# Where the first expert's weights are loaded among attention's loads

## The chip, the cores and the metric

The kernel runs on one core of a Trainium2 chip. The metric is device time in microseconds (us) of one execution, given as the median over the runs.

## What is computed

An mLSTM cell over 4 batches, 8 heads, 768 positions and head size 40, and behind it a layer of 8 experts to which each position is sent by a hash of its token. All is float32. The reference, cut:

```python
for t in range(S):                       # per batch and head
    m_new  = maximum(f_gate[t] + m, i_gate[t])
    f_stab = exp(f_gate[t] + m - m_new); i_stab = exp(i_gate[t] - m_new)
    C = f_stab * C + i_stab * outer(v[t], k[t])
    n = f_stab * n + i_stab * k[t]
    y[t] = sigmoid(o_gate[t]) * (C @ q[t]) / maximum(abs(n @ q[t]), 1.0)
x = y.transpose(0, 2, 1, 3).reshape(3072, 320)
expert = token_ids * 2654435761 % 8
for e in range(8):
    out[expert == e] = maximum(x[expert == e] @ w1[e], 0) @ w2[e]   # w1[e] 320x1024, w2[e] 1024x320
```

## The kernel before, in words

The 3072 positions are 24 tiles of 128; tile s belongs to batch s % 4 and chunk s // 4. Attention is one loop over 24 steps (L810). It is written under a manual schedule: each engine carries out its instructions in the order in which the program names them, and so does SyncE with the loads that it issues.

The recurrence is done by chunks. For a tile, PE turns k and q (`turn`, L390), multiplies them to scores (`scores`, L447), and makes the decays from the gate rows R and the row ends L (`decays`, L405, and xb, L418). ACT takes their exponential (L414), DVE multiplies scores and decays (`weigh`, L453). `state` (L478) makes the chunk's part of the state C, `attend` (L499 and L505) the output, which DVE divides (`divided`) and POOL multiplies with the output gate (`gated`, L522). ACT works out the output gate (`gate`, L438 and L439).

The work is staggered: step s turns tile s + 2, makes the scores and decays of tile s + 1 and attends tile s. The gate of tile i is worked out in step i + 1 for i of 8 and more.

SyncE's queue holds nearly all loads. In step s, in this order: the gate rows R of tile s + 3 (`load_a`, L248; 24 KB, three buffers), k and q of tile s + 5 and v of tile s + 4 (L237; 160 KB each, in pieces of 160 bytes, six buffers each), in each fourth step the ends L, the output gate og of tile s + 1 (L233; 160 KB, pieces of 160 bytes; early in the loop sometimes two of them), and the stores of finished rows x (L525; 160 KB). Then come the "pieces" of the step (L846): small parts of the routing, and the loads of the first expert's weights. From tile 17 on, the x rows are stored from POOL's queue.

`slices_of(0)` (L120) makes seven pieces for the first expert's weights: two halves of w1t (512 KB each, 128 rows of 4 KB; L131), w1c (two loads of 128 KB; L134), and four slices of w2t (320 KB each; L137). Their tiles belong to expert 0 alone at this time, so nothing has to be free before they are loaded. Behind the loop, L901 uses w1t and w1c (`layer1` of the rows of two gathered tiles, L157 and L150), and the second block uses w2t (`layer2`, L1030).

After attention, POOL gathers the rows of each expert from the stored x, the rows go through `x_slots` to the turned blocks, and the experts 1 to 7 follow, each with its own loads of weights (L97 to L101).

Of the kernel before, what the change touches and what calls it, by code (L numbers as in the profile page):

```python
# [22 lines left out]
def kernel(  # L23
# [96 lines left out]
    def slices_of(e):  # L120

        w1t = wpools[0].tile([P, 2, F], F32, name="w1t")
        w1c = wpools[0].tile([P, FB // 2, P], F32, name="w1c")
        w2t = w2pools[0].tile([P, FB, Dm], F32, name="w2t")
        W[e] = w1t, w1c, w2t
        last = moe_w1[e][2 * P :, :].rearrange("d (a two f) -> two d a f", two=2, f=P)
        rows = moe_w2[e].rearrange("(a p) d -> p a d", p=P)

        def part(i):
            if i < 2:  # L130
                nc.sync.dma_start(w1t[:, i], moe_w1[e][i * P : (i + 1) * P, :])  # L131
            elif i == 2:
                for j in range(2):
                    nc.sync.dma_start(w1c[j * P // 2 : (j + 1) * P // 2], last[j])  # L134
            else:
                r = slice(2 * (i - 3), 2 * (i - 2))
                nc.sync.dma_start(w2t[:, r], rows[:, r])  # L137

        return [lambda i=i: part(i) for i in range(7)]
# [50 lines left out]
    with tc.tile_pool(name="gates", bufs=1) as gp, \  # L190
# [363 lines left out]
        def route_iotas(i):  # L554
            for ti, tf, pattern, base, mult in list(iotas.values())[i::2]:
                nc.gpsimd.iota(ti[:], pattern=pattern, base=base, channel_multiplier=mult)
                nc.gpsimd.tensor_copy(tf[:], ti[:])
# [140 lines left out]
        def route_table(i):  # L698
            tk = ps.tile([P, 2, NC], F32, name="tk", tag="sp0")
            for t in range(TH):  # L700
                nc.tensor.matmul(tk[:], lhsT=oh_r[:, t, :], rhs=oh_c[:, t], start=(t == 0), stop=(t == TH - 1))
            for part in range(2):
                if i == 0 and part == 0:
                    nc.vector.tensor_copy(tv[:], tk[:, 0])
                else:
                    nc.vector.tensor_tensor(tv[:], tv[:], tk[:, part], op=ALU.add)

        def route_index():
# [17 lines left out]
        pieces = {  # L726
            2: [lambda: route_iotas(0)], 3: [lambda: route_iotas(1), route_consts, route_parts], 4: [route_experts],
            5: [route_chosen], 7: [route_extra, route_masked], 8: [route_rank], 9: [route_high], 10: [route_slots, g2.ends, lambda: g2.split("e")], 11: [route_places],
            20: [route_index], 21: [route_tiles],
        }  # L730
        products = {4: [route_turned], 5: [route_counts]}
        for i in range(8):
            pieces.setdefault(12 + i, []).append(lambda i=i: route_hot(i))
            if i % 2:
                products[12 + i] = [lambda i=i // 2: route_table(i)]
        for i, part in enumerate(slices_of(0)):
            pieces.setdefault(17 + i, []).append(part)
        gates_of = {}
        for i, j in enumerate((4, 5, 6, 6, 7, 8, 8, 9)):
            gates_of.setdefault(j, []).append(i)  # L740
# [356 lines left out]
    with tc.manual_schedule():  # L1097
# [56 lines left out]
        for e in range(E):  # L1154
            g, i = e // EG, e % EG
# [84 lines left out]
```

## Time and profile before

| | us |
|---|---|
| median of 6 runs | 357.03 (354.9 to 361.04) |
| profiled execution, its own time | 359.1 |
| its span, first to last instruction | 357.1 |
| PE busy | 338.6 (95%) |
| DVE, ACT, POOL busy | 226.8, 138.4, 213.7 |
| attention's loop, about | 10 to 130 |
| first layer of expert 0 | 130 to 140 |
| experts 1 to 7 | 162 to 337 |

Time is counted from the start of the span. In a timeline or chain, a line holds the start, the duration, the engine and line number; "SPq" is an issue in SyncE's queue, "DMA" a transfer's flight, "issue" time in which the profile shows no wait. In square brackets stands the idle time before an instruction and what ended it. A table by stretches of time gives the busy time of PE, PE's weight loads, DVE, ACT and POOL, then the granted PE clock (1.00 is full), the DMA share of the 16 engines and the GB/s. The DMA share sums the time of packets, which can overlap, so it can pass 1.

The trace also keeps each transfer's semaphore events: each DMA engine that takes part counts one up when its part has landed.

### The profile page before, as it was taken

To read this page: it belongs to the slowest core of one execution; us is meant where nothing else is said; L and a number is where in the kernel's file an instruction comes from. 1 tells how busy PE (TensorE), PEld (TensorE's weight loads), DVE (VectorE), ACT (ScalarE), POOL (GpSimd) and SP (SyncE) were. 2 spreads that over 40 slices of the span, in tenths; PEclk is the share of its full clock that TensorE was granted. 3 is DMA by queue.
4 is the path that set the end of the run, shared out by engine and by line. 5 is a ranking of instruction groups with operands and counts; after the bars stand their busy time and mean duration, and the time that the engine had idled before them with its cause. 6 is when DMAs were issued, how large, how long until landed. Compare 5 with 4: busy or idle time off the path is not lost.

```text
span 357.1 us, 9206 instructions
## 1 busy us (share of the span) xinstructions
PE 338.6 (95%) x3573; PEld 291.8 (82%) x3573; DVE 226.8 (64%) x512; ACT 138.4 (39%) x325; POOL 213.7 (60%) x301
## 2 busy tenths in 40 slices
PE   6889999999999799999999999999999999999990
PEld 5677898888888677788899899689899899898870
DVE  8867897998888551056765786826666757645310
ACT  6676688776675351113213212212313212213200
POOL 8832778899885546407717938816917829329221
PEclk9999999999999899999999999999999999999997
DMA  6699999999999963689878869495585592010010
GB/s 128 116 174 172 174 187 176 194 190 184 172 181 245 228 203 110 174 230 288 239 208 238 272 104 366 107 247 177 118 239 194 115 265 99 0 37 19 17 39 3
DMA packets 162358, 59.18 MB, mean 166 GB/s; under 512 B 140171, under 2 KB 158119, under 8 KB 162313
## 3 DMA queue, kind: packets, MB, share of 16 engines
q1 hardware_dynamic: 158377, 49.05, 59.0%
q0 software_dynamic: 2832, 9.34, 8.0%
q8 instruction: 29, 0.48, 0.6%
q10 hardware_dynamic: 1104, 0.18, 0.3%
q14 instruction: 16, 0.13, 0.1%
HBM read 46.48 MB, written 12.38 MB: 165 GB/s over the span
## 4 chain that ended last, share of the span: by engine, by line
PE 77%; DMA 6%; issue 5%; DVE 4%; SPq 3%; POOL 2%; ACT 1%; ACTq 0%; POOLq 0%; DVEq 0%
PE mh L988 20%; PE mh L1063 13%; PE zp L1030 8%; PE mh L996 6%; PE sp L447 6%; PE tr L390 5%; PE xh L505 5%; PE xh L499 3%; PE ab L405 3%; PE xh L478 2%; SPq L1125 2%; DMA R<-gate_rows 2%; DMA w1t<-in_moe_w_dram 2%; PE zp L1143 1%; DMA xg<-x_rows,g_idx 1%
## 5 line engine op out<-in xcount | busy, mean ns | idle before, releaser
L914 POOL DMA_INDIRECT out_dram<-zo,s_idx x26 | 27.3, 1051 | 76.7 <-issue 47.1
L1030 PE MATMUL zp<-w2t,h 128*128 128x320 f32 x160 | 45.0, 433 | 0.5 <-ACT h L166 0.5
L974 DVE TENSOR_TENSOR h<-u,mh 128x416 f32<-128x416 f32 (+1 forms) x56 | 25.5, 475 | 25.0 <-PE mh L988 12.7
L1030 PEld LDWEIGHTS zp<-w2t,h 128*128 128x128 f32 x160 | 30.0, 190 | 11.8 <-ACT h L166 0.9
L505 PE MATMUL xh<-v,w 128*64 128x41 f32 x768 | 35.7, 226 | 0.0
L414 ACT ACTIVATE w<-ab 128x512 f32<-128x512 f32 x48 | 26.2, 596 | 19.6 <-PE ab L405 18.7
L453 DVE TENSOR_TENSOR w<-sp,w 128x512 f32<-128x512 f32 x48 | 30.8, 682 | 3.8 <-ACT w L414 3.8
L988 PE MATMUL mh<-tx,sw 128*128 128x208 f32 x168 | 31.9, 340 | 0.5 <-DVE sw L944 0.5
L505 PEld LDWEIGHTS xh<-v,w 128*64 128x64 f32 x768 | 31.8, 141 | 0.0
L988 PEld LDWEIGHTS mh<-tx,sw 128*128 128x128 f32 x168 | 29.7, 190 | 0.9 <-DVE sw L944 0.9
L447 PE MATMUL sp<-qT,kT 64*128 64x128 f32 x384 | 28.3, 286 | 1.1 <-ACT qT L395 1.1
L110 POOL DMA_INDIRECT xg<-x_rows,g_idx x24 | 23.3, 972 | 9.0 <-issue 6.7
L499 PE MATMUL xh<-C,qs 128*64 128x82 f32 x320 | 28.2, 254 | 0.0
L447 PEld LDWEIGHTS sp<-qT,kT 64*128 64x128 f32 x384 | 23.7, 189 | 5.0 <-issue 2.5
L1063 PE MATMUL mh<-tw,sh 128*128 128x160 f32 x168 | 27.4, 299 | 0.0
L522 POOL TENSOR_TENSOR x<-x,og 128x320 f32<-128x320 f32 x24 | 20.6, 864 | 10.4 <-ACT og L439 8.3
L974 DVE TENSOR_TENSOR u<-m,mh 128x416 f32<-128x416 f32 x28 | 16.5, 588 | 13.3 <-ACT m L1002 6.8
L1012 ACT ACTIVATE h<-mh 128x416 f32<-128x416 f32 x14 | 7.2, 518 | 44.3 <-PE mh L996 44.3
L1063 PEld LDWEIGHTS mh<-tw,sh 128*128 128x128 f32 x168 | 24.3, 190 | 0.0
L988 PE MATMUL mh<-xT,w1t 128*128 128x208 f32 x112 | 24.3, 339 | 0.0
L996 PE MATMUL mh<-xT,w1c 64*128 64x208 f32 x224 | 23.5, 349 | 0.0
L488 POOL TENSOR_TENSOR C<-C,add 64x164 f32<-64x164 f32 x32 | 16.3, 508 | 9.9 <-ACT add L482 8.7
(241 smaller groups left out, 758.1 us busy)
## 6 DMA issues: line engine op xcount, KB each, us to landing
w2t<-in_moe_w_dram SPq DMA_DIRECT2D x7, 1280.0 KB
w1t<-in_moe_w_dram SPq DMA_DIRECT2D x7, 1024.0 KB
xb<-x_slots SPq DMA_DIRECT2D x84, 52.0 KB
k<-in_k_dram SPq DMA_DIRECT2D x24, 160.0 KB
v<-in_v_dram SPq DMA_DIRECT2D x24, 160.0 KB
og<-in_o_gate_dram SPq DMA_DIRECT2D x24, 160.0 KB
q<-in_q_dram SPq DMA_DIRECT2D x23, 160.0 KB
x_slots<-xg SPq DMA_DIRECT2D x7, 480.0 KB
```

The costliest lines, as they stand in the source:

```text
L110: nc.gpsimd.indirect_dma_start(out=xg, out_offset=None, in_=x_d[:rows, :], in_offset=bass.IndirectOffsetOnAxis(ap=idx, axis=0),)
L414: nc.scalar.activation(w[:, hf], ab[:], AF.Exp)
L447: nc.tensor.matmul(sp[hf][:, j, :], lhsT=d["kT"][r, j, :], rhs=d["qT"][r, j, :], start=True, stop=True)
L453: nc.vector.tensor_tensor(d["w"][:, hf], d["sp"][hf][:], d["w"][:, hf], op=ALU.mult)
L499: nc.tensor.matmul(xh[t, 2 * j : 2 * j + 2, :], lhsT=d["qs"][:, j, t], rhs=Cs[b][c % 2][:, j].rearrange("p h d -> p (h d)"), start=True, s ...
L505: nc.tensor.matmul(hs[t, 2 * j + hf, :], lhsT=d["w"][:, hf, j, t], rhs=d["v"][:, 2 * j + hf, :], start=(c == 0), stop=True, skip_group_che ...
L914: ins = nc.gpsimd.indirect_dma_start(out=out[:, :], out_offset=bass.IndirectOffsetOnAxis(ap=idx, axis=0), in_=zo[:], in_offset=None, bound ...
L974: nc.vector.tensor_tensor(o, a, b, op=ALU.add)
L988: nc.tensor.matmul(pair(bank[n])[:, a], lhsT=lhsT(g + a), rhs=rhs, start=first and a == 0, stop=True, skip_group_check=True,)
L996: nc.tensor.matmul(pair(bank[n])[:, a], lhsT=w1c[k, g + a, :], rhs=xT[k, 2, r], start=False, stop=True, skip_group_check=True,)
L1030: nc.tensor.matmul(zp[:], lhsT=h[:, fb, j * P : (j + 1) * P], rhs=w[2][:, fb, :], start=(fb == 0), stop=(fb == FB - 1),)
L1063: nc.tensor.matmul(bank[n], lhsT=lhsT(f), rhs=rhs(f), start=first and f == 0, stop=f == FB // 2 - 1, skip_group_check=True,)
```

## The change

The seven pieces go to other steps: the two w1t halves from steps 17 and 18 to 2 and 9, w1c from 19 to 15, and the four w2t slices from 20, 21, 22 and 23 to 21, 21, 22 and 22. In SyncE's queue this puts the first w1t half ahead of tile 6's R, the second ahead of tile 13's, w1c ahead of tile 19's, and all w2t slices behind the last og load. The order of the instructions on ACT and POOL stays the same.

```diff
-        for i, part in enumerate(slices_of(0)):
-            pieces.setdefault(17 + i, []).append(part)
+        for s, part in zip((2, 9, 15, 21, 21, 22, 22), slices_of(0)):
+            pieces.setdefault(s, []).append(part)
```

## The prediction

> **What bounds it now.** I read the page first (PE is busy 95% of the span and holds 77% of the chain), then the chain of waits, because the edit touches only SyncE's queue and matters only where a transfer ends a PE wait. In all of attention the waits of PE name one such place; the chain, around it:
>
> ```profile
> 110.78 0.47 PE tr L390 x4
> ...
> 112.35 0.51 SPq L233
> ...
> 112.96 0.59 SPq L525
> ...
> 113.61 0.47 SPq L131
> ...
> 114.17 5.42 DMA R<-gate_rows
> 119.59 0.04 issue
> 119.64 0.62 PE ab L405 x4
> ```
>
> Here PE, in step 21, waits for the gate rows R of tile 22. They were issued at 114.17, straight behind the second w1t slice (L131), and took 5.42 us to land. PE's timeline puts the price on it, and the table by stretches shows what comes after:
>
> ```profile
> 115.96 1.27 PE L447 MATMUL sp<-qT,kT 64*128 64x128 f32 x16
> 119.64 0.62 PE L405 MATMUL ab<-R,L 128*64 128x512 bf16 x4 [2.40 <-DMA R<-gate_rows]
> ...
> 124.53 0.62 PE L405 MATMUL ab<-R,L 128*64 128x512 bf16 x4
> ```
>
> ```profile
> 118.00:119.60 1.60, 0.00 (x0) 0.00 (x0) 0.43 (x3) 0.00 (x0) 1.10 (x2) 1.00 0.85 194
> ...
> 121.60:122.60 1.00, 1.00 (x22) 1.00 (x21) 0.88 (x2) 0.71 (x2) 0.17 (x1) 0.50 0.87 157
> ```
>
> After 2.40 us of idle the granted clock (the third column from the right) is 0.50. From decays to the end of attend, step 20 took 2.25 us (112.69 to 114.94) and step 21, at half clock, 3.60 (119.64 to 123.24): 1.35 more; the following scores take 1.29 in the chain where others take 1.09: 0.20 more. So the stall costs 2.40 + 1.35 + 0.20 = **3.95 us**, all on the chain. No other wait of PE stands between 35 and 126 us.
>
> The second thing to know is how full the transfers are before that:
>
> ```profile
> 30.00:55.00 25.00, 24.82 (x481) 21.22 (x479) 22.32 (x58) 18.13 (x45) 16.51 (x25) 1.00 0.98 178
> 55.00:80.00 25.00, 25.00 (x500) 21.93 (x498) 22.42 (x49) 19.47 (x50) 22.20 (x41) 1.00 0.93 189
> 80.00:105.00 25.00, 25.00 (x500) 21.94 (x496) 20.80 (x53) 16.94 (x41) 21.95 (x37) 1.00 0.93 182
> 105.00:130.00 25.00, 22.14 (x400) 19.28 (x396) 17.94 (x54) 14.53 (x35) 13.63 (x20) 0.93 0.98 244
> ```
>
> The last two columns are DMA share and GB/s: 0.93 to 0.98 long before the weights come. SyncE's waits for consumers in the whole kernel are small in attention (the largest groups: 2.5 us on ACT's og, 1.8 and 1.7 on POOL), so its queue runs as fast as the transfers let it, and not as fast as PE lets it. Then a queue that is full works first in, first out: bytes put in early push back everything behind them and that push is not won back.
>
> **Spare time at each R.** Each load counts up its semaphore as its parts land; the last count, from the trace's semaphore events, is its landing. Set against the start of the decays matmuls (L405) in PE's timeline, R lands ahead of its need by: tile 6 4.7 us (34.30 against 39.01), tile 9 6.3 (47.46, 53.78), tile 12 3.6 (64.76, 68.36), tile 13 2.65 (70.54, 73.19), tile 18 2.35 (95.46, 97.81), tile 19 2.8 (100.04, 102.87), tile 20 3.06 (104.64, 107.70), tile 21 1.1 (111.58, 112.69), behind the first w1t; tile 22 is late, 119.59 against 117.24, where PE was ready. The spare time falls from 6.3 to 2.65 between tiles 9 and 13 without any weights, in the steps with two og loads or two stores; afterwards it stays near 2.8, so the queue neither gains nor loses on PE's 4.9 us a step.
>
> **The edits.** No instruction is added on any engine; the order of the queue alone changes, and each moved piece issues what it did (one load per w1t and w2 slice, two for w1c). SyncE's issue of a w1t, 0.42 to 0.47 us, moves with it.
>
> What a moved piece costs where it goes: the median landings of the loads on both sides of the two w1t's in before give 2.5 us (issued at 107 us) and 1.5 us (114 us) above the same loads without one, and the two w1c's together 3.6, of which an instruction fetch (16 KB, 1.05 us at 116.9) held one of the engines for 1.1: 2.5. From below, the 320 KB w2 slices at the end of attention land 0.85 to 0.92 us apart, which scaled by bytes is 1.4 for a w1t and 0.7 for the w1c pair. From further below, nothing, if idle transfer time takes it; rival B has that. I take 1.4 for step 2, since the share at 32 to 34 us is 0.72; 2.0 for step 9, the mean of the two measured; 1.6 for w1c at step 15, between its bounds. The push is then 1.4 from step 3, 3.4 from step 10, 5.0 from step 16, where before it was 2.5 from step 18, 4.0 from 19 and 6.5 from 20.
>
> Removed: R of tile 22 no longer has a w1t straight ahead of it. Added, R by R (landing of before plus the difference of pushes): tile 13 at 73.94, PE 0.75 late; tile 18 at 98.86, 1.05 late; tile 19 at 100.04 + 5.0 = 105.04, 2.17 late; tile 20 1.94; tile 21 at 111.58 + 5.0 - 2.5 = 114.08, 1.39; tile 22 at 119.59 + 5.0 - 4.0 = 120.59, 3.35 behind a PE that never waited; tile 23 at 123.28 - 1.5 = 121.78, 0.2 (needed 4.33 after tile 22, step 20's length). PE's lateness is the largest of these, since it does not catch up: 3.35 us, taken in stalls of 0.75, 0.3, 1.1 and 1.2. With all costs as measured (6.5 in sum) it is 3.7 at tile 19 and 4.85 at tile 22. Against 3.95 of before, the change is worth -0.6 to +0.9.
>
> The clock belongs to this sum: a stall of 2.40 us halved it, the 1.0 us that PE lacks in each of the stretches 8 to 10 and 12 to 14 us did not (1.00 there), so I charge nothing for stalls of up to 1.2, and 1.55 (1.35 + 0.20) for each one that comes near 2.4. The Trainium skill ("TensorE: Matmul & The Clock Gate", section "HAM oscillation") speaks of gaps over about 3.4 us before the clock halves; the trace shows it after 2.40, so the row decides. By the rule the 1.55 could not come back even in one stall of 2.2, and the sum would stay at its plain value.
>
> w2: in the queue only the first slice moves, behind the last two og loads. The slices landed at 125.8 to 131.9 and are first used by layer 2 at 140.62: 8.7 us of cover, and the two og loads gain the slice's 0.9 us, for which nothing waits. If the cover went, layer 2 would wait for a slice of 0.9 us. The gathers on POOL at 118.79 wait for the store of tile 16, which the queue issued at 112.96; the push of 5.0 instead of 2.5 delays it to 115.5 and its landing (115.91) to 118.4, still before them. After attention everything hangs on its end (x, store, gathers, x_slots, w1t of expert 1 at 154.56): a shift passes through one to one.
>
> **Sum and rivals.** Case A (0.47): the stall moves and is paid in parts, -0.6 to +0.9, middle +0.15. With step 9 and w1c at 1.4 too (4.2 in sum) tile 22 is 2.55 late and the change worth -1.4; the middle with one half-clock window is +1.7. The profiled execution took 359.1 us (span 357.1), 2.1 over the median of 357.03; the same shift on the median gives **357.2**, own range 355.6 to 358.7.
>
> Case B (0.27), faster: the transfers have room. For it: 244 GB/s in the last stretch, with weights, against 178 to 189 before, and a share of 0.93 in the middle, 0.07 of 50 us or 3.5 us idle, which about covers 3.4. Then R of tiles 13 to 22 stays early and the 3.95 us go: 353.1; half of it would be 355.1. Against it: the spare time did not grow in steps 13 to 20, with only six loads each. [...]
>
> Case C (0.26), slower: the output gate, not R, is first. og lands behind R in each step and ACT takes it in order: of tile 16 it landed at 99.59 and was used at 99.64, of tile 17 at 103.84 and 104.70. With the pushes as measured, tile 17's lands at 110.34, 5.6 late; ACT idles 0.75 before the next kT copy, so the copy, and PE behind it, is 4.9 late, and one stall long enough to halve the clock makes 6.4, against 3.95: +2.5, 359.5. It decides from a push of 5.6 at step 16 (3.95 + 0.86 + 0.75), or of 4.0 if the stall halves the clock. Against it: R's matmuls come before og's use in the step, and a kT is read a step later. That the edit does nothing is excluded: the loads' order in SyncE's queue differs as the diff says, and ACT's and POOL's do not.
>
> **The numbers.** A lies inside 0.5% (1.8 us, about what a measurement of this kernel can tell from no change); B is faster, C slower: 0.27, 0.47 and 0.26. The range goes down to B's 353.1 and up past C's 359.5 by most of a second half-clock window (1.1 of 1.55), which leaves out less than 0.2: 353.0 to 360.6.
>
> **What would show it.** Right: PE waits of 0.5 to 2 us for R (or ACT for og) between 70 and 106 us, no half clock or a shorter one near 120, decays of tile 23 within 1 us of 124.53, the chain through R or og loads earlier than step 18. For B: no PE wait after 31 us, decays of tile 23 near 120.6. For C: ACT's gate (L438) waiting for og from 75 us, PE's transposes or copies late behind it. The step most likely wrong is the cost of a w1t beside attention's loads, and that pushes add up undiminished.

## The result, and the profile after

The changed kernel takes 360.88 us (median; 357.48 to 363.96) against 358.02 us (354.90 to 361.04) for the kernel before on the same chips: a ratio of 1.0079, 95% interval 1.0062 to 1.0096. It is slower by 0.8%, 2.8 us at that ratio. The forecast of 357.2 us and no difference is wrong; the slower case stood at 0.26 with 359.5. The profiled execution took 361.02 us (span 359.1), close to its median.

The first views are PE's and ACT's waits in attention and after it (total, times, longest), with the lines that are new or gone.

```profile
PE tpx L747 <- DMA xg<-x_rows,g_idx: 2.0, 1, 2.0
PE tk L701 <- POOL oh_c L690: 0.7, 1, 0.7
```

```profile
ACT w L414 <- PE ab L405: 11.9, 17, 1.8
ACT og L438 <- DMA og<-in_o_gate_dram: 4.3, 6, 1.7
```

The same two lists held before:

```profile
PE ab L405 <- DMA R<-gate_rows: 2.4, 1, 2.4
```

```profile
ACT og L438 <- DMA og<-in_o_gate_dram: 0.4, 1, 0.4
```

The wait for R is gone from PE's list, and nothing in it waits for R at any other tile. In its place PE waits 2.0 us for the second of the two gathers of expert 0's rows, and 0.7 for POOL; ACT, which before waited 0.4 us in all for an output gate, now waits 4.3 us in six places. PE's timeline shows the first half of the exchange as a gain and the second as a loss:

```profile
113.93 0.62 PE L405 MATMUL ab<-R,L 128*64 128x512 bf16 x4
118.47 0.62 PE L405 MATMUL ab<-R,L 128*64 128x512 bf16 x4
122.68 0.62 PE L405 MATMUL ab<-R,L 128*64 128x512 bf16 x4
...
127.94 0.87 PE L747 MATMUL tpx<-ident,xg 128*128 128x128 f32 x3 [2.00 <-DMA xg<-x_rows,g_idx]
131.71 3.32 PE L157 MATMUL mh<-xT,w1t 128*128 128x256 f32 x8
```

Decays of tile 21 start 1.24 us later than before (113.93 against 112.69), those of tile 23 1.85 us earlier (122.68 against 124.53), since no stall of 2.40 us stands between. Then comes the wait for the gather, and behind it eight matmuls take 3.32 us. The table by stretches (granted clock in the third column from the right) says why:

```profile
122.00:125.00 3.00, 3.00 (x67) 2.48 (x63) 1.93 (x4) 1.77 (x5) 1.83 (x3) 1.00 0.99 327
125.50:127.50 2.00, 0.43 (x3) 0.20 (x2) 0.05 (x1) 1.50 (x4) 1.37 (x2) 1.00 0.92 330
127.60:131.00 3.40, 3.06 (x41) 2.76 (x43) 1.12 (x5) 1.03 (x3) 1.43 (x2) 0.50 0.15 55
131.00:134.40 3.40, 3.40 (x20) 2.81 (x19) 1.02 (x4) 0.00 (x0) 0.94 (x2) 0.50 0.13 48
```

From 122 to 127.5 us the transfers run at 327 to 330 GB/s with PE nearly idle in the last two us; then the clock is at half for 6.8 us. From decays of tile 23 to expert 1 (its first matmul, L988) the kernel before needs 36.09 us (124.53 to 160.62), this execution 40.52 (122.68 to 163.20): 4.4 lost there. So in these two profiles 1.85 is won and 4.4 lost.

The chain tells what holds the gather, and also where the lateness of tile 21 comes from:

```profile
103.40 2.95 DMA og<-in_o_gate_dram
106.35 1.68 issue
108.03 0.87 POOL x L522
...
110.06 0.74 POOL C L458
110.80 0.38 POOL oh_c L690
...
111.73 0.29 PE tk L701 x3
...
121.37 6.44 DMA xg<-x_rows,g_idx
...
127.94 0.87 PE tpx L747 x3
```

The chain runs through the output gate of tile 17, as case C said: og landed at 106.91, ACT used it at 106.93 (in the profile before, landed at 103.84, used at 104.70), POOL's product with it (L522) and what POOL does behind it were late, and PE's routing product (tk) and the turns behind it with them. The second gather was issued at 121.37 and needed 6.44 us. POOL's timelines, after and then before, give the issue of both gathers:

```profile
120.01 1.05 POOL L110 DMA_INDIRECT xg<-x_rows,g_idx  x1 [0.50 <-DMA og<-in_o_gate_dram]
121.37 0.97 POOL L110 DMA_INDIRECT xg<-x_rows,g_idx  x1 [0.30 <-issue]
```

```profile
118.79 1.05 POOL L110 DMA_INDIRECT xg<-x_rows,g_idx  x1 [0.50 <-DMA v<-in_v_dram]
120.14 0.97 POOL L110 DMA_INDIRECT xg<-x_rows,g_idx  x1 [0.31 <-issue]
```

They go out 1.2 us later than before (ahead of them in POOL's order stands the product with tile 19's gate, which started at 117.78, before at 116.56), and SyncE issued the four w2 slices, 1.28 MB, from 119.99 to 121.73, three of them in front of the second one; before, the first slice was issued at 120.92, behind both gathers, and the others from 124.10 on. By their semaphore events the gathers land at 125.26 and 127.81, before at 122.71 and 124.36.

The landings of R (last count), after minus before, against the pushes that were forecast (the loop itself starts 0.4 us later in the profile after: decays of tile 3 at 24.79 for 24.41):

| R of tile | 6 | 9 | 12 | 13 | 18 | 19 | 20 | 21 | 22 | 23 |
|---|---|---|---|---|---|---|---|---|---|---|
| forecast | 1.4 | 1.4 | 1.4 | 3.4 | 3.4 | 5.0 | 5.0 | 2.5 | 1.0 | -1.5 |
| measured | 1.4 | 0.9 | 0.0 | 1.0 | 1.1 | 2.8 | 2.0 | 0.0 | -1.9 | -3.0 |

### The profile page after: what moved, and what is told of

Read it like the earlier page. It is cut to its first block, busy times and chain, and to the rows that moved or that the text cites. A ratio compares the mean times of both kernels' runs of the same rounds, so it can differ in the third digit from the quotient of the medians.

```text
span 359.1 us, 9206 instructions
## 1 busy us (share of the span) xinstructions
PE 340.3 (95%) x3573; PEld 293.0 (82%) x3573; DVE 227.5 (63%) x512; ACT 138.6 (39%) x325; POOL 213.8 (60%) x301
## 4 chain that ended last, share of the span: by engine, by line
PE 79%; DMA 6%; issue 5%; SPq 2%; DVE 2%; POOL 2%; ACT 1%; ACTq 0%; POOLq 0%
PE mh L988 20%; PE mh L1063 13%; PE zp L1030 12%; PE mh L996 6%; PE sp L447 5%; PE tr L390 4%; PE mh L157 4%; PE xh L505 4%; DMA og<-in_o_gate_dram 3%; PE xh L499 2%; PE ab L405 2%; PE xh L478 2%; DMA xg<-x_rows,g_idx 2%; SPq L237 1%; PE zp L1143 1%
## 5 line engine op out<-in xcount | busy, mean ns | idle before, releaser
L914 POOL DMA_INDIRECT out_dram<-zo,s_idx x26 | 27.5, 1057 | 76.9 <-issue 46.8
L988 PE MATMUL mh<-tx,sw 128*128 128x208 f32 x168 | 31.9, 340 | 0.0
L988 PEld LDWEIGHTS mh<-tx,sw 128*128 128x128 f32 x168 | 29.7, 190 | 0.3 <-DVE sw L944 0.3
L522 POOL TENSOR_TENSOR x<-x,og 128x320 f32<-128x320 f32 x24 | 20.6, 863 | 12.5 <-ACT og L439 4.5
L988 PE MATMUL mh<-xT,w1t 128*128 128x208 f32 x112 | 24.3, 339 | 0.0
L996 PEld LDWEIGHTS mh<-xT,w1c 64*128 64x128 f32 x224 | 19.0, 186 | 3.5 <-issue 3.5
```

What stands on the lines that cost most here:

```text
L914: ins = nc.gpsimd.indirect_dma_start(out=out[:, :], out_offset=bass.IndirectOffsetOnAxis(ap=idx, axis=0), in_=zo[:], in_offset=None, bound ...
L988: nc.tensor.matmul(pair(bank[n])[:, a], lhsT=lhsT(g + a), rhs=rhs, start=first and a == 0, stop=True, skip_group_check=True,)
L996: nc.tensor.matmul(pair(bank[n])[:, a], lhsT=w1c[k, g + a, :], rhs=xT[k, 2, r], start=False, stop=True, skip_group_check=True,)
```

## The experiments

The theory after the result, **T**: the gathers behind the bunched w2 slices cost the time (2.0 us of wait and a half clock). The rival, **W**: the early w1 pushes the output gates, ACT and POOL come late, and PE with them. (The first two expectations set T against another rival, that the new places of w2 cost the time by themselves.) Each ratio is to the kernel before, run on the same chip beside it, with its 95% interval. Each edit is to the changed kernel unless it says otherwise. What follows attention differs between profiles by several us for one and the same kernel (from expert 1 to the end 196.5 and 202.3 us in the two profiles of the kernel before), so single profiles are compared in attention alone, and the whole by ratios.

### Only w1 moved, only w2 moved

```diff
-        for s, part in zip((2, 9, 15, 21, 21, 22, 22), slices_of(0)):
+        for s, part in zip((2, 9, 15, 20, 21, 22, 23), slices_of(0)):
```

> Only w1 moves (2, 9, 15); w2 stays in steps 20 to 23. Theory (w2 slices, now early, stand ahead of the two gathers of expert 0's rows in the DMA engines): SyncE's queue is early by itself, so w2 still comes before the gathers; PE still waits 1 to 2 us for a gather near 127 us and the time is 1.004 to 1.009 of before, like the full change. Rival (the new places of w2 make the loss): the wait goes and the time is 0.990 to 0.996.

Measured: 1.0019 (0.9990 to 1.0048). No wait for the gather, ACT's waits for og are the largest:

```profile
ACT og L438 <- DMA og<-in_o_gate_dram: 10.6, 9, 2.6
```

PE waited twice for R, 1.1 us in all, and once 0.7 for POOL; decays of tile 23 started at 124.46, as late as before's with its stall.

```diff
-        for s, part in zip((2, 9, 15, 21, 21, 22, 22), slices_of(0)):
+        for s, part in zip((17, 18, 19, 21, 21, 22, 22), slices_of(0)):
```

> Only w2 moves (steps 21 and 22); w1 stays in 17 to 19. Theory: the queue is late as before, w2 is issued near 124 us behind the gathers, so within 0.3% of before, the wait for R of tile 22 still there (about 2.4 us), none for a gather. Rival (the new places of w2 make the loss): 1.005 to 1.012.

Measured: 1.0003 (0.9965 to 1.0042), no wait for the gather, and 0.5 us for R, where 2.4 was expected. The slices went out at 122.19 to 123.93, behind both gathers (119.63 and 120.98), as T had it for this kernel. What follows: neither half costs what the whole does. w2 bunched does no harm while the gathers go out ahead of it, which T allows; with only w1 moved one slice (119.82) stood ahead of the gathers, and the wait of 1 to 2 us that T expected there did not come. w1 early costs little while w2 is spread, so W alone is short.

### w2 taken out of SyncE's queue

```diff
-                nc.sync.dma_start(w2t[:, r], rows[:, r])
+                nc.scalar.dma_start(w2t[:, r], rows[:, r])
...
-        for s, part in zip((2, 9, 15, 21, 21, 22, 22), slices_of(0)):
+        parts = slices_of(0)
+        for s, part in zip((2, 9, 15), parts):
             pieces.setdefault(s, []).append(part)
...
+        for part in parts[3:]:
+            part()
```

(the slices go out from ACT, behind the loop and ahead of the first layer.)

> w1 in steps 2, 9 and 15; the w2 slices are issued from ACT's queue behind the last step, when the gathers of xg0 have landed. Theory: PE waits neither for R nor for a gather, no half clock between 117 and 135 us, 3 to 5 us less than before (0.986 to 0.992). Rival (late og loads, pushed by w1, hold POOL's gathers): the gather is still issued after 121 us and PE waits 1 us or more; 0.997 to 1.005.

Measured: 1.0166 (1.0119 to 1.0214). Both theories missed. The slices now leave at 129.8 to 131.2 us and collide with the last x stores, which land 3 to 4 us later; the gathers of the other experts wait for them (138.3 instead of about 135), PE waits 1.9 us in the second block and 1.7 for a w1t, and expert 1 starts at 164.09. The edit made a collision of its own and tells nothing of T.

The same with w1 back in steps 17, 18 and 19:

```diff
-        for s, part in zip((2, 9, 15), parts):
+        for s, part in zip((17, 18, 19), parts):
```

> w1 in steps 17, 18 and 19 as before, w2 on ACT's queue behind the last step. Theory: the wait for R of tile 22 stays, and before has no wait for a gather, so within 0.4% of before (0.997 to 1.003). Rival (w2 beside the last loads costs time in before too): 0.990 to 0.996.

Measured: 1.0067 (1.0022 to 1.0111). The stores are late here too, in a profiled execution of 364.93 us, 3.7 over the median of this kernel. So w2 behind the loop costs some 0.7% by itself, and early w1 another 1.0% beside it (1.0166 against 1.0067), where it cost 0.2% with w2 in SyncE's queue: the costs do not add up.

```diff
-                nc.sync.dma_start(w2t[:, r], rows[:, r])
+                nc.scalar.dma_start(w2t[:, r], rows[:, r])
...
-        for s, part in zip((2, 9, 15, 21, 21, 22, 22), slices_of(0)):
+        for s, part in zip((2, 9, 15, 23, 23, 23, 23), slices_of(0)):
```

> w1 in steps 2, 9 and 15; w2 issued from ACT's queue in step 23 (about 126 to 128 us), behind the two gathers of xg0 and ahead of the last store of x rows. Theory (w2 in the DMA engines ahead of the gathers makes the loss): no PE wait for a gather over 0.5 us, last store of x rows in flight under 3 us, 0.994 to 1.000 of before, and at least 0.6% under the full change. Rival (w1's early place makes the loss by pushing og and with it POOL): 1.003 to 1.009, like the full change.

Measured: 1.0075 (1.0046 to 1.0104). The gathers flew 3.2 and 3.0 us and nothing waited for them, but ACT's four issues stand in front of its copy xT:

```profile
PE mh L157 <- ACT xT L748: 1.9, 1, 1.9
```

Those 1.9 us are 0.5% of the 0.75. Attention itself was not late (decays of tile 23 at 121.84), with the same w1: ACT's waits for og were 1.6 us here and 10.6 with w1 moved alone. How late og comes differs from execution to execution.

### The gather given more time, or w2 earlier still

```diff
+            attend(s)
...
-            attend(s)
```

(in step 23 PE's turns of the gathered rows, which stood ahead of `attend`, come behind it.)

> The full change, but in step 23 PE attends (1.2 us) before it turns the second gathered tile, so that a late gather costs 1.2 us less and PE is idle for less. Theory: the PE wait for the gather falls from 2.0 us to 0.8 or less, no half clock there, 1 to 3 us less than the full change (0.999 to 1.005 of before). Rival (the gather is not what costs): within 0.3% of the full change (1.005 to 1.011).

Measured: 1.0041 (1.0021 to 1.0061). No wait for the gather in the profile (in flight 4.6 and 5.9 us). Some of the loss goes, not all of it.

```diff
-        for s, part in zip((2, 9, 15, 21, 21, 22, 22), slices_of(0)):
+        for s, part in zip((2, 9, 15, 4, 11, 13, 17), slices_of(0)):
```

> w1 in steps 2, 9 and 15 and the four w2 slices in steps 4, 11, 13 and 17: nothing of the weights behind step 17. Theory: the gathers find the DMA engines free (in flight under 4 us) and PE doesn't wait for them; og of tiles 12 to 19 lands 1 to 2 us later than with the full change, so 0.995 to 1.003 of before. Rival (pushed og loads make the loss): more of them, 1.008 to 1.015.

Measured: 1.0077 (1.0051 to 1.0104), with the gathers in flight for 3.4 and 3.0 us. PE's and ACT's waits:

```profile
PE ab L405 <- DMA R<-gate_rows: 3.6, 4, 1.5
```

```profile
ACT og L438 <- DMA og<-in_o_gate_dram: 10.0, 9, 1.9
```

The gather is free here, and the kernel is as slow: 1.28 MB more ahead of R and og made both late, and decays of tile 23 start at 126.59. This is W without T, with more bytes ahead than the change has, and in the longest of the six executions (363.89 us).

### w1c back in step 19

```diff
-        for s, part in zip((2, 9, 15, 21, 21, 22, 22), slices_of(0)):
+        for s, part in zip((2, 9, 19, 21, 21, 22, 22), slices_of(0)):
```

> The full change, but w1c in step 19 as before. Theory (gathers behind w2): og of tiles 16 to 18 earlier by 1 to 2 us, w2 later by as much, small: 1.002 to 1.008. Rival (w1c's push on og of tiles 16 to 18 makes the loss: ACT waited 1.75 us for tile 17's): the loss goes, 0.996 to 1.001.

Measured: 1.0016 (1.0001 to 1.0031). ACT's waits for og fall to 2.5 us, decays of tile 23 start at 122.42 and nothing waits for the gathers. So the 256 KB of w1c at step 15 belong to the loss: they come six steps behind the second w1t, whose push is not yet worked off (R of tile 18, issued just ahead of w1c, still lands 1.1 us later in the table above).

```diff
-        for s, part in zip((2, 9, 15, 21, 21, 22, 22), slices_of(0)):
+        for s, part in zip((2, 9, 19, 20, 21, 22, 23), slices_of(0)):
```

> Only the two w1t halves move (steps 2 and 9); w1c and w2 stay as before. Rival (pushed og loads): w1c at step 15 was the push that counted, so 0.994 to 1.000. Theory (gathers behind w2): the queue is early at the end as with the full change, so 1.001 to 1.006.

Measured: 1.0000 (0.9981 to 1.0020). Both w1t halves early, everything else in its old step: no loss, and no gain either, although no wait for R is in its profile.

### The two kernels again, and the gathers ahead of POOL's gate

The kernel before and the changed one were run again on one chip, with the last experiment above and this:

```diff
+            if s == NT - 4:
+                for j in range(2):
+                    gather(xg0[:, j, :Dm], g_idx[:, j : j + 1], TE * P)
...
-            if s == NT - 4:
-                for j in range(2):
-                    gather(xg0[:, j, :Dm], g_idx[:, j : j + 1], TE * P)
```

(in step 20 POOL issues the two gathers ahead of its product with the output gate.)

> The kernel before, unchanged, beside the full change on one chip: 0.998 to 1.002. Its profile tells how much the lengths of attention and of the gathers' flight differ from one execution to the next: decays of tile 23 within 1.5 us of 124.5 expected, gathers 4 to 4.5 us in flight.

Measured: 0.9997 (0.9977 to 1.0016). PE's timeline of the kernel before, a second execution:

```profile
112.51 0.62 PE L405 MATMUL ab<-R,L 128*64 128x512 bf16 x4
116.98 0.62 PE L405 MATMUL ab<-R,L 128*64 128x512 bf16 x4
121.79 0.62 PE L405 MATMUL ab<-R,L 128*64 128x512 bf16 x4
```

The decays of tile 23 were expected within 1.5 us of 124.5 and start at 121.79. From the decays of tile 21 to those of tile 22 it takes 4.47 us, against 6.95 in the profile that the prediction was made from (112.69 to 119.64), and no half clock follows. **The stall that the change was to remove is not in every execution of the kernel before.** The mean clock of each execution speaks of it too: of the 27 compared executions of the kernel before beside the first four experiments, 15 had 0.991 or more (median 357.38 us) and 12 had 0.986 to 0.990 (359.78); in this series 32 of 35 had 0.991 or more. A half-clock window of 3.4 us in a span of 357 is 0.005 of mean clock. Over all five series of the kernel before, 99 of 126 had 0.991 or more. The mean clock is no mark of this one stall, though: the second profiled execution had 0.989 itself, and its half clock stands at about 195.5 to 199 us, among the experts. So the count says how many executions can have had the stall with its half clock at most; a stall without one it does not see (2.3 us for R with og loaded first, below).

> The full change, unchanged: 1.006 to 1.010. Theory (gathers behind w2): a gather over 5.5 us in flight and a PE wait for it of 1 us or more in this profile too. Rival (pushed og loads): ACT's waits for og sum to 5 us or more, the decays of tile 23 stand later than in the kernel before on this chip, and PE waits less than 0.5 us for a gather.

Measured: 1.0057 (1.0033 to 1.0082). Here 11 of 12 executions had a mean clock of 0.991 or more, and their median, 361.76, is 1.8 us over the 359.94 of the kernel before at such a clock. So the two half-clock windows of the first profile after are not what a usual execution pays: in its own series, too, only 4 of 34 executions had a mean clock of 0.983 or less, as it had (0.982), and 16 had 0.991 or more. The profiled execution of this run is the fastest of its twelve (360.10). In it the wait for the gather is 0.3 us, where T expected 1 or more; ACT's waits for og sum to 3.5, where W expected 5; and decays of tile 23 start 0.66 later than in the kernel before on the same chip, as W expected.

> The full change, but POOL issues the two gathers of step 20 ahead of gating tile 19, so they neither wait for ACT's gate of tile 19 nor stand behind w2. Theory: gathers issued near 117.5 us, 3 to 4.5 us in flight, no PE wait for them, 0.997 to 1.003. Rival (pushed og loads reach PE through ACT and the copies): gathers early, but within 0.3% of the full change, 1.005 to 1.010.

Measured: 1.0016 (0.9995 to 1.0037). The profiled execution is the slowest of its twelve (362.81). ACT waited 8.4 us for og in it and attention ended late (decays of tile 23 at 124.89). The gathers were expected near 117.5; they went out at 120.71 and 122.07, behind 3.61 us in which POOL was idle, flew 4.7 and 5.9 us, and PE did not wait for them. By the ratio most of the loss is gone with the gathers ahead of a late gate. In what way, this profile does not show: the gathers go out later than in the first profile after, and fly only 0.5 us shorter.

### The output gate loaded first, and w2 on POOL's queue

If og is what comes late, it can be put ahead of k, q and v in SyncE's queue:

```diff
+            for i in gates_of.get(s + 2, ()) if s + 2 < NT - 1 else gates_of[NT - 1] if s == NT - 3 else ():
+                load(i, "o")
...
-            for i in gates_of.get(s + 2, ()) if s + 2 < NT - 1 else gates_of[NT - 1] if s == NT - 3 else ():
-                load(i, "o")
```

> The full change, and in each step og is loaded ahead of k, q and v, so that a push by w1 doesn't reach it. Rival (pushed og loads make the loss): ACT waits less than 1 us in all for og, no late POOL, 0.994 to 1.000. Theory (gathers behind w2): og on time, but the gathers still meet w2, over 5 us in flight, 1.002 to 1.007.

Measured: 1.0035 (1.0002 to 1.0068). PE's and ACT's waits:

```profile
PE ab L405 <- DMA R<-gate_rows: 2.3, 1, 2.3
```

```profile
ACT og L438 <- DMA og<-in_o_gate_dram: 0.3, 1, 0.3
```

ACT no longer waits, and R is late instead: the same bytes, another payer.

```diff
-                nc.sync.dma_start(w2t[:, r], rows[:, r])
+                nc.gpsimd.dma_start(w2t[:, r], rows[:, r])
...
-        for s, part in zip((2, 9, 15, 21, 21, 22, 22), slices_of(0)):
+        for s, part in zip((2, 9, 15, 21, 21, 21, 21), slices_of(0)):
```

(the slices go out from POOL, behind its gathers.)

> The full change, but w2 is issued from POOL's queue in step 21, right behind the two gathers, and so can't stand ahead of them. Theory (gathers behind w2): gathers under 4.5 us in flight, PE waits less than 0.3 us for them, 0.997 to 1.002. Rival (pushed og loads): ACT still waits 3 us or more for og and the loss stays, 1.004 to 1.009.

Measured: 1.0106 (1.0066 to 1.0145). The gathers flew 3.2 and 3.0 us, unhindered, and the kernel is no faster. PE's waits, with R:

```profile
PE ab L405 <- DMA R<-gate_rows: 1.4, 1, 1.4
PE tpx L747 <- DVE xg L886: 0.8, 1, 0.8
PE tk L701 <- POOL oh_c L690: 0.7, 1, 0.7
PE mh L157 <- ACT xT L748: 0.7, 1, 0.7
```

POOL's four issues (3.0 us in all) delay what POOL does behind them, which would explain the two lines through DVE xg and ACT xT; ACT waited 9.2 us for og. (R was late at tile 19, at 104.63, long before the slices went out at 123.61 to 125.81.) This too has a cost of its own, so it refutes T as the only payer without measuring W.

Both edits together:

> Both: og ahead of k, q and v, and w2 on POOL behind the gathers. If the two theories share the loss, this is the fastest, 0.990 to 0.998; if one of them has it all, within 0.2% of that one's own kernel.

Measured: 1.0038 (1.0010 to 1.0067). R was late twice, 3.1 us in all, with a half-clock window at 76.9. And og loaded first in the kernel before, as a control:

> The kernel before with og ahead of k, q and v, weights in their old places. og in before is nearly late only (0 to 1 us of spare time), so both theories say little: 0.997 to 1.002; less than 0.995 would say that og bounds before too.

Measured: 1.0010 (0.9981 to 1.0039), R late twice (3.5 us), a half clock at 122.2. The order of og and k, q, v alone changes nothing that can be told.

### Two more executions of the changed kernel

> The changed kernel once more, unaltered, for the profile of another execution. The loss of the median execution is +1.8 to +2.8 us; of the executions so far 11 of 12 in one series ran at a mean clock of 0.991 or more, so without a half-clock window in attention. If the gathers behind w2 pay the loss, this profile shows PE waiting for xg by 1 us or more and expert 1 starting 2 us or more behind its decays of tile 23 plus 36. If the output gate pays it, the decays of tile 23 start at 123.5 or later, ACT waits for og by 8 us or more, and no wait for xg stands there.

Measured: 1.0050 (1.0027 to 1.0074); the profiled execution took 360.02 us, the second fastest of its eight.

> A second look of the same kind: the same two alternatives with the same numbers, a wait for xg of 1 us or more against decays of tile 23 at 123.5 or later. If both looks show neither, the loss of a median execution lies where single profiles of attention do not show it, and the split stays open.

Measured: 1.0059 (1.0007 to 1.0112); the profiled execution took 360.64, the median of its series, against 359.41 for the kernel before. Its ACT timeline at the gate of tile 17, and then PE's at the routing product:

```profile
107.36 0.47 ACT L438 ACTIVATE og<-og 128x320 f32<-128x320 f32 x1 [2.18 <-DMA og<-in_o_gate_dram]
```

```profile
112.17 0.29 PE L701 MATMUL tk<-oh_c,oh_r 128*128 128x94 bf16 x3 [0.72 <-POOL oh_c L690]
```

The chain is that of the first profile: og late by about 2 us, then POOL, then PE. Set out over all profiles of the two kernels:

| | before | before again | after | again | third | fourth |
|---|---|---|---|---|---|---|
| decays, tile 20 to 21 | 5.06 | 5.07 | 5.94 | 5.85 | 5.96 | 6.20 |
| decays, tile 12 to 23 | 56.24 | 53.68 | 54.02 | 54.31 | 54.38 | 54.72 |
| longest wait of ACT for og | 0.4 | none | 1.7 | 1.6 | 1.8 | 2.2 |
| PE's wait for the gather | none | none | 2.0 | 0.3 | 0.8 | none |
| decays of tile 23 to expert 1 | 36.09 | 36.09 | 40.52 | 36.09 | 36.28 | 36.10 |

All four executions of the changed kernel lose 0.8 to 1.1 us in the one step in which POOL is behind a late og, and win only 0.1 to 0.5 of it back by tile 23 (second row; 53.5 to 53.7 also in the profiles with only w2 moved, with w2 on ACT in step 23 and with w1c back). At the gather one of the four pays much, one 0.2, two nothing (last row). So my expectation's numbers for the gate (8 us of waits, decays of tile 23 at 123.5) were too high; its mechanism stands in all four profiles. It does not tell a slow kernel from others by itself: in the one profile that each of them has, the step from tile 20 to 21 took 6.23 us with only w1 moved (1.0019), 6.11 with the gathers first (1.0016) and 5.58 with both w1t halves alone (1.0000).

## Why the prediction was wrong, point by point

**The stall of before, 3.95 us on the chain, was read rightly and carried wrongly.** It is in the profile, and the changed kernel does not have it: from tile 12 to tile 23 the profile after needs 2.2 us less. But the step "the profiled execution took 359.1 us, 2.1 over the median; the same shift on the median gives 357.2" put the removal of a stall on a median that mostly does not have it, as far as one more profile and the mean clocks tell. Against the execution without it (53.68) the changed kernel has nothing to win and loses 0.3 to 1.0. That the profiled time stood 2.1 us over the median was a sign, in view and used only as an offset. (The starts of the decays that the working sets against the landings for tiles 6 to 20 are 0.07 us later than the timeline has them, 107.70 for 107.63; no term moves by more.)

**"Pushes add up undiminished" failed.** The first w1t cost R of tile 6 the 1.4 us that were forecast, and by tile 12 the queue had won them back. From tile 13 the push is 1.0 in place of 3.4, behind w1c at most 2.8 in place of 5.0. Before had a DMA share of 0.93 between 55 and 80 us; the stretch after holds it at 0.98 (205 GB/s for 189): the gaps took the first weights, as case B argued. The prediction called this the step most likely wrong; it was, but the time did not follow, because R was not the first load to be late.

**Case A named the wrong load.** R was late in none of the four profiles. The forecast's stalls of 0.75, 1.1 and 1.2 us for R did not come.

**Case C had the mechanism and not the size.** og of tile 17 is the one that it named; it was to be 5.6 late and cost 4.9 and a half clock. It landed 3.1 us later, ACT waited 1.75 (2.2 in another execution), and the step cost 0.8 to 1.1, without a half clock. The route to PE was also another: not by the kT copy read a step later, but by POOL's product with the gate and the one-hot (oh_c) that PE's routing product waits for 0.7 us. I looked only at ACT's own output and did not follow POOL behind it.

**"w2 ... 8.7 us of cover" and gathers "still before them" failed.** The cover was counted for the slices' own use; what stands behind the slices is a second user, the gathers on POOL's queue. They were 1.2 us later, the slices earlier, and the flight of the second grew from 4.2 to 6.44 us. The step priced at nothing cost 4.4 in the first profile, 0 to 0.2 in three others. The Trainium skill ("DMA: Bandwidth & Descriptors", "Rules for kernel authors") says that issuing from other engines' queues brings no bandwidth, as all run on the same 16 engines; the longer flight of POOL's gathers beside SyncE's 1.28 MB agrees with it, and so does w2 on ACT's queue behind the loop, where the last x stores landed 3 to 4 us later.

**The clock:** idle times of 1.2 us and less were to cost no half clock. Between 20 and 130 us that held in every profile, up to 1.48 us. Elsewhere it did not: the second profile of the kernel before has a window of half clock that starts at about 195.5 us, behind

```profile
195.09 1.36 PE L988 MATMUL mh<-tx,sw 128*128 128x208 f32 x4 [1.22 <-DVE h L974]
```

and 0.87 to 1.10 us of idle at 13 us stand before one in three other profiles (w2 alone, w2 on ACT behind the loop with early w1, gathers first), where 0.96 us in the profile before gave none. 2.00 us at the gather gave two windows at half speed, 6.8 us, where 2.40 at R had given one of 3.4. It is no sharp bound: 2.3 us at R (og loaded first) and 1.9 at xT (w2 on ACT in step 23) gave none; 2.6, 2.7 and 3.7 one each. The skill's 3.4 us ("TensorE: Matmul & The Clock Gate", "HAM oscillation") is longer than all but the last of the idle times that sufficed here.

**What is shown and what is open.** Shown, by ratios: three edits each take most of the loss away. They put w1c back in step 19 (1.0016), spread w2 again (1.0019), or issue the gathers of expert 0 ahead of POOL's gate (1.0016), against 1.0050 to 1.0079 for the whole in its four measurements; only the last of the three was run beside the whole. So w1c as early as step 15, w2 bunched, and the gathers behind the gate make the loss together. Seen in all four profiled executions: a late og, through ACT and POOL, costs 0.8 to 1.1 us in one step. For the execution that was the median of its series, 1.2 us over the kernel before, that would be most of the loss. But that it is the payer is not shown, as kernels that lose 0.2% or nothing have a long step there as well; and where the loss was 1.8 us, or 2.8 as in the first series, the rest is open. The gather can pay it, at 4.4 us in one execution of four, but how often it does cannot be read from times alone. No version was faster than the kernel before by more than its interval; the best, both w1t halves early and the rest in place, was 1.0000.

## What to carry to other kernels

Ask of a stall in a profile whether it is in the median execution, for only what is in most executions can be won there: a profiled time well above the median is a warning, and further profiles tell. In a queue that is nearly full, ask for every load behind the moved bytes when it is used and by whom, down the chain of engines (here og, ACT, POOL, PE), and not only for the load that was late before. Price a bunch of transfers by what starts beside it on any queue, not by its own first use.

## What the runs showed of the hardware

The issue of a load by SyncE is not of constant length: in the profile after half of the 136 issues between 20 and 125 us take under 0.58 us, but 20 take 1 us or more, as x_rows at 96.96 (1.69), k at 104.84 (1.07) and v at 110.97 (1.93). Each of these three overlaps an instruction fetch, one packet of 16 KB that takes 1.0 to 1.1 us (at 97.12, 104.40 and 110.92). There are 15 such fetches in that time, one every 5 to 8 us; 14 of the 20 long issues overlap one, and 13 of the 116 shorter ones. That the fetch is the cause was not tried.

The flight of the two indirect gathers of 128 rows differs with the loads beside them. With early w1 and no w2 slice near them (w2 on ACT's or POOL's queue, or far earlier) they took 3.0 to 3.6 us in five profiles; in the two profiles of the kernel before 3.9 to 4.9; in the four of the changed kernel, beside 1.28 MB of loads from another engine's queue, 3.9 to 5.3 for the first and 4.8 to 6.4 for the second.
